# Second batch of a local-attention and token-mixer kernel: half of x, and the first pair, turned by VectorE and DMA; weights of the token map split ahead of x, low halves shared with VectorE

## The chip, the cores and the metric

The kernel runs on one core of a Trainium2 chip. The metric is device time in microseconds: 560.84 us for the kernel before, the median of 3 runs (560.51 to 561.32). The profile is of one execution; its times are counted from the start of its span. Engines: PE is TensorE (PEld its weight loads), DVE VectorE, ACT ScalarE, POOL GpSimd, SP the queue that issues every DMA of this kernel.

## The reference

Windowed attention with summary keys for 4 batches of 8 heads, and behind it a mixer block: one linear map pair across the 768 tokens, one across the 512 channels.

```
scores_l = q @ k.T / 8, masked to |i - j| < 16         # per batch and head, S = 768, D = 64
scores_s = q @ blockmax32(k).T / 8 + log(32)
a = softmax([scores_l, scores_s]);  x = a @ [v, blockmean32(v)]     # heads side by side: 768 x 512
h = relu(x.T @ w_tok1) @ w_tok2                        # 768 -> 256 -> 768 along the tokens
u = x + h.T
out = u + relu(u @ w_ch1) @ w_ch2                      # 512 -> 1536 -> 512 along the channels
```

## The kernel before

**Tiles.** Heads go in pairs: pair p of batch b has number 4 b + p (names such as k_7 or av_16 count pairs or heads over all batches, others count batch, half and pair: up_1_0_2 is batch 1, half 0, pair 2). A batch's tokens fall into two halves, 512 and 256 wide (384 and 384 in the last batch). x lies with tokens on the partitions, x2 holding two pairs of heads; the mixer across channels needs u with channels on the partitions. So x must be turned somewhere between.

**Precision.** Every large product is made of three: an operand is split into a high part (ACT, a copy to a shorter form) and a low part (a subtraction on POOL or DVE), and high x high, high x low and low x high are summed in PSUM.

**Steps of a batch.** `scores` (sc) and `lowest`/`power` give e; `turn` turns e on PE in batches 0 and 1, `turn_blocks` does it in batches 2 and 3 with one 32x32 transpose on DVE, a write to DRAM (away) and four fetches (eT); `weighted` (av) gives x2. The first token map (t1q) runs in `tok1x` for batch 1, two pairs at a time, and in `tok1_all` for batches 2 and 3. `tok2` is the second token map (up): in batches 0 and 1 it first turns x on PE against an identity, into the same PSUM bank, four 128x128 pieces for half 0 and two for half 1; in batches from FAR = 2 on, x comes turned through `turn_x` (DVE transpose xb, write xaway) and `fetch_x` (four fetches xT), and DVE adds the PSUM result to it. `ch1` (hp) and `ch2` (acc) are the channel maps, twelve blocks f of twelve matmuls each for either half, `finish` adds u and writes out.

**Order.** Batch b's channel maps run while batch b+1's attention runs between them. Every piece of work is handed to a `Plan` with an engine, an assumed duration, what it reads and writes, and a rank; the planner plays them through and writes each engine's instructions in the order that comes out. So a change of durations or needs moves instructions on all five engines. Each engine then executes its list strictly in that order, waiting on semaphores. SP issues the DMAs in order too, and a DMA there may also wait until an older DMA has landed.

**Buffers.** A slot has a tag with so many buffers, taken in turn; the first writer of a slot waits until the users of the slot that many places before it are done. Those that matter here: `e` (3), `u0` (4), `ot` (2), and `vb` (1), whose loads in_vb are summed by DVE into vs_2, the block means of batch 2. In PSUM, `att` has two banks; in half 0 the scores, weighted sums and second token map of the next batch share these two, in half 1 they also use acc2 and acc3.

Of the kernel before, what the change touches and what calls it, by code (L numbers as in the profile page):

```python
# [21 lines left out]
DTOK = 256  # L22
# [177 lines left out]
def tile_attention_mixer(  # L200
# [443 lines left out]
    def att_step(b, s, behind=()):  # L644

        kind, hp, g = (LATER if b >= FAR else ORDER)[s]
        p = b * NP + hp
        if kind == "e":
            (turn_blocks if b >= FAR else turn)(p, g)
        elif kind == "a":  # L650
            weighted(p)
            if b >= FAR:
                turn_x(b, hp)
            ahead = 1 if b > 0 else 2
            if b > 0 or hp + ahead < NP:
                load_v(2 * (p + ahead))
                load_v(2 * (p + ahead) + 1)
        else:
            scores(p, g, behind)
            if b == 0 and g == 1:  # L660
                first_means(p)
            if g == 0 and p != NP - 1:
                key_blocks(p + 1)
            if g == 1 and p + 2 < (NP if b == 0 else B * NP):
                load_k(p + 2)
                state["q"] = load_q(p + 2)
# [4 lines left out]
    def turn_x(b, p):  # L671

        x2, a = x_t[b, p]
        e = sbuf([P, S], "e", f"xb_{b}_{p}", 3)
        add(
            "dve", 1.05,
            lambda: nc.vector.transpose(
                e.t.rearrange("p (r t s) -> p t r s", r=P // 32, s=32),
                x2.t[:, :, a, :].rearrange("p t (r s) -> p t r s", s=32),
            ),  # L680
            reads=x_keys(b, p), writes=[(e, 0)], rank=R_ATT,
        )
        away = xa_t[b, p] = plan.slot(dram, [P, S], F32, "xaway", f"xaway_{b}_{p}", 8)
        add(
            "sp", 0.4, lambda: nc.sync.dma_start(out=away.t, in_=e.t),
            reads=[(e, 0)], writes=[(away, 0)], kb=393,
        )

    def fetch_x(b, half, p):
        nt, away = HT[b][half], xa_t[b, p]  # L690
        ts = slice(H0[b][half] // P, (H0[b][half] + nt) // P)
        if b == B - 1:
            slot, behind = sums_at(half, p), state["turned"]
        else:
            tag, bufs = (("e", 3), ("ot", 2))[half]
            slot = xT_t[b, half, p] = sbuf([P, nt], tag, f"xT_{b}_{half}_{p}", bufs)
            behind = ()
        fetch(
            away, slot,
            lambda rows: away.t.rearrange("(q p) (r t s) -> p r q t s", p=32, r=P // 32, s=32)[  # L700
                :, rows.start // 32, :, ts
            ],
            from_sources, nt // 8, behind,
        )
# [114 lines left out]
    def tok1_all(b):  # L819

        pts = [att_bank(f"t1q_{b}_{k}") for k in range(DTOK // P)]
        xk = [key for p in range(NP) for key in x_keys(b, p)]
        for T in range(TT):
            if T % 2 == 0:
                ws = sbuf([P, 2, 2, DTOK], "u0", f"ws_{b}_{T}", 4, F32R)
                split(ws, lambda ws=ws: (ws.t[:, 0], ws.t[:, 1]), [
                    lambda T=T: (slice(None), wt1.t[:, T : T + 2])
                ], [(wt1, T // 2)])
            xs = sbuf([P, 2, NP, P], "u0", f"xs_{b}_{T}", 4, F32R)
            split(xs, lambda xs=xs: (xs.t[:, 0], xs.t[:, 1]), [  # L830
                lambda T=T, g=g: (slice(2 * g, 2 * g + 2), x2_t[b, g].t[:, T]) for g in range(2)
            ], xk)

            def products(T=T, xs=xs, ws=ws):
                for k, pt in enumerate(pts):
                    for i, (wp, xp) in enumerate(((0, 0), (0, 1), (1, 0))):
                        nc.tensor.matmul(  # L837
                            pt.t.rearrange("p (a c) -> p a c", c=P),
                            lhsT=ws.t[:, wp, T % 2, k * P : (k + 1) * P], rhs=xs.t[:, xp],
                            start=(T == 0 and i == 0), stop=(T == TT - 1 and i == 2),  # L840
                        )

            add(
                "pe", 1.37, products, reads=[(s, i) for s in (xs, ws) for i in range(2)],
                writes=[(pt, 0) for pt in pts], rank=R_ATT,
            )
        for p in range(NP):
            t1 = t1_t[b, p] = sbuf([P, 2, DTOK], "t1", f"t1_{b}_{p}", 4, F32R)
            for k, pt in enumerate(pts):
                cs = slice(p * P, (p + 1) * P)  # L850
                to = slice(k * P, (k + 1) * P)
                add(
                    "act", 0.3,
                    lambda t1=t1, pt=pt, cs=cs, to=to: nc.scalar.activation(
                        t1.t[:, 0, to], pt.t[:, cs], AF.Relu
                    ),
                    reads=[(pt, 0)], writes=[(t1, (0, k))], rank=R_EVAC,
                )
                add(
                    "dve", 0.3,  # L860
                    lambda t1=t1, pt=pt, cs=cs, to=to: nc.vector.scalar_tensor_tensor(
                        out=t1.t[:, 1, to], in0=pt.t[:, cs], scalar=0.0,
                        in1=t1.t[:, 0, to].bitcast(F32), op0=ALU.max, op1=ALU.subtract,
                    ),
                    reads=[(pt, 0), (t1, (0, k))], writes=[(t1, (1, k))], rank=R_EVAC,
                )

    def split(slot, parts, sources, keys):

        for source in sources:  # L870
            add(
                "act", 0.62 / len(sources),
                lambda source=source: nc.scalar.activation(
                    parts()[0][:, source()[0]], source()[1], AF.Copy
                ),
                reads=keys, writes=[(slot, 0)], rank=R_EVAC,
            )
        for source in sources:
            add(
                "pool", 1.3 / len(sources),  # L880
                lambda source=source: nc.gpsimd.tensor_tensor(
                    out=parts()[1][:, source()[0]], in0=source()[1],
                    in1=parts()[0][:, source()[0]].bitcast(F32), op=ALU.subtract,
                ),
                reads=keys + [(slot, 0)], writes=[(slot, 1)], rank=R_EVAC,
            )

    def t1_keys(b, p):
# [877 lines left out]
    for b in range(B - 1):  # L1766
# [11 lines left out]
        for slot, (half, f) in enumerate(seq):  # L1778
            state["phase"] = half
            for p in range(NP):  # L1780
                if b >= FAR and u1s[p] == slot + 2:
                    fetch_x(b, 1, p)
                if u1s[p] == slot:
                    tok2(b, 1, p)
# [39 lines left out]
                tok1x(b + 1, t1s.index(slot))  # L1824
            for p in range(NP):
                if slot == t2s[p]:
                    if b + 1 >= FAR:
                        fetch_x(b + 1, 0, p)
                    tok2(b + 1, 0, p)
            if b + 2 == B and slot == 23:  # L1830
# [66 lines left out]
```

## Time and profile before

| | |
|---|---|
| median of 3 runs | 560.84 us |
| the profiled execution | 559.61 us |
| its span, first to last instruction | 557.8 us |
| mean granted TensorE clock | 1.000 |
| POOL busy | 246.8 us (44%) |
| DMA, mean over the span | 181 GB/s, 101.10 MB |
| batch 0's channel maps, from hp_0_0_0 | 64.2 us |
| batch 1's, from hp_1_0_0 | 199.7 us |
| batch 2's, from hp_2_0_0 | 330.7 us |
| last batch's, from z | 466.6 us |

The page gives busy time by engine and the costliest groups of instructions (line, engine, operation, out<-in, count, busy us, mean ns). Rows of a timeline have the start in us, the length in us, engine, line, operation and tiles, a count where neighbours are merged, and in brackets the idle time before it and what ended it. Matmuls overlap in the pipeline, so the length of one is its latency; what it costs is the distance to the next start. Rows of a wait view have engine and line, what was waited for, us in sum, times, and the longest. Rows of the windows view have the stretch, then busy us and instruction count of PE, PEld, DVE, ACT and POOL, the granted clock, the DMA share and GB/s.

### The profile page before, as it was taken

To read this page: it belongs to the slowest core of one execution; us is meant where nothing else is said; L and a number is where in the kernel's file an instruction comes from. 1 tells how busy PE (TensorE), PEld (TensorE's weight loads), DVE (VectorE), ACT (ScalarE), POOL (GpSimd) and SP (SyncE) were. 2 spreads that over 40 slices of the span, in tenths; PEclk is the share of its full clock that TensorE was granted. 3 is DMA by queue.
4 is the path that set the end of the run, shared out by engine and by line. 5 is a ranking of instruction groups with operands and counts; after the bars stand their busy time and mean duration, and the time that the engine had idled before them with its cause. 6 is when DMAs were issued, how large, how long until landed. Compare 5 with 4: busy or idle time off the path is not lost.

```text
span 557.8 us, 12595 instructions
## 1 busy us (share of the span) xinstructions
PE 544.0 (98%) x4557; PEld 479.6 (86%) x4557; DVE 330.3 (59%) x922; ACT 251.9 (45%) x784; POOL 246.8 (44%) x362
## 2 busy tenths in 40 slices
PE   7699999999999999999999999999999999999997
PEld 4588788888999978888799988878889999999997
DVE  4788999979365355454543247454352065669992
ACT  4786666625585344332323325343433453356410
POOL 0326687835574932310067404378769963000000
PEclk9999999999999999999999999999999999999999
DMA  8963668755668138768595316787696543932742
GB/s 277 330 189 108 215 209 249 240 163 190 203 187 251 42 131 226 198 207 226 146 253 137 104 29 196 160 237 198 171 259 168 135 155 116 333 95 81 219 134 85
DMA packets 125743, 101.10 MB, mean 181 GB/s; under 512 B 70000, under 2 KB 105456, under 8 KB 125680
## 3 DMA queue, kind: packets, MB, share of 16 engines
q1 hardware_dynamic: 125680, 100.29, 60.7%
q8 instruction: 36, 0.59, 0.5%
q14 instruction: 27, 0.22, 0.1%
HBM read 70.18 MB, written 28.31 MB: 177 GB/s over the span
## 4 chain that ended last, share of the span: by engine, by line
PE 90%; ACT 4%; DVE 3%; POOL 2%; issue 1%; ACTq 0%
PE acc L1024 27%; PE hp L981 27%; PE sc L467 4%; PE av L599 4%; PE up L920 3%; PE t1q L837 3%; ACT e L491 2%; PE x L1251 2%; PE y L1251 2%; PE z L1251 2%; PE pz L1251 2%; PE t1q L800 2%; PE up L1213 2%; PE warm L1731 1%; PE pw L1251 1%; PE pv L1251 1%
## 5 line engine op out<-in xcount | busy, mean ns | idle before, releaser
L1024 PE MATMUL acc<-h,w2h 128*128 128x256 f32 (+1 forms) x576 | 153.8, 339 | 0.0
L981 PE MATMUL hp<-u,w1h 128*128 128x256 f32 (+1 forms) x576 | 143.8, 339 | 0.0
L1024 PEld LDWEIGHTS acc<-h,w2h 128*128 128x128 f32 x576 | 100.6, 188 | 13.8 <-ACT h L993 1.6
L981 PEld LDWEIGHTS hp<-u,w1h 128*128 128x128 f32 x576 | 98.0, 189 | 12.4 <-issue 1.1
L981 PE MATMUL hp<-u,w1l 128*128 128x256 f32 (+1 forms) x288 | 96.9, 336 | 0.0
L491 ACT ACTIVATE e<-e,den 128x120 f32<-128x120 f32 x192 | 73.3, 384 | 52.0 <-DVE den L481 39.1
L1024 PE MATMUL acc<-h,w2l 128*128 128x256 f32 (+1 forms) x288 | 96.4, 335 | 0.0
L998 DVE SCALAR_TENSOR_TENSOR h<-hp,h 128x512 fp32r<-128x512 f32 (+1 forms) x72 | 39.9, 554 | 90.9 <-ACT h L993 90.7
L993 ACT ACTIVATE h<-hp 128x512 fp32r<-128x512 f32 (+1 forms) x72 | 35.2, 489 | 114.7 <-PE hp L981 114.5
L981 PEld LDWEIGHTS hp<-u,w1l 128*128 128x128 f32 x288 | 54.4, 189 | 5.8
L1024 PEld LDWEIGHTS acc<-h,w2l 128*128 128x128 f32 x288 | 54.2, 188 | 5.2
L481 DVE CUSTOM_DVE_ANT_0 e<-sc,mask_sb 128x120 f32<-128x120 f32 x192 | 41.7, 277 | 16.8 <-PE sc L467 16.2
L605 POOL TENSOR_SCALAR rec<-den 128x6 f32<-128x6 f32 x32 | 8.6, 269 | 66.1 <-ACT e L491 64.0
L491 ACT ACTIVATION_READ_ACCUMULATOR e<-e,den 128x1 f32 x192 | 36.1, 188 | 0.0
L1064 POOL TENSOR_TENSOR ot<-ot,u 128x512 f32<-128x512 f32 (+1 forms) x24 | 24.4, 1042 | 19.7 <-DVE ot L1056 18.2
L467 PE MATMUL sc<-k,q 64*64 64x120 f32 x768 | 28.0, 271 | 3.7 <-DVE den L481 2.2
L467 PEld LDWEIGHTS sc<-k,q 64*64 64x64 f32 x768 | 20.5, 132 | 12.5 <-issue 6.2
L920 PE MATMUL up<-wt2h,t 128*128 128x512 f32 (+1 forms) x96 | 28.4, 354 | 0.6 <-DVE t L739 0.6
L599 PEld LDWEIGHTS av<-v,eT 120*64 120x64 f32 x768 | 24.0, 138 | 4.7 <-issue 2.8
L599 PE MATMUL av<-v,eT 120*64 120x64 f32 x768 | 26.5, 224 | 0.9 <-PE hp L981 0.4
L335 DVE TENSOR_REDUCE ks<-k 128x24 f32<-128x768 f32 x16 | 15.2, 948 | 20.5 <-DMA k<-in_kw 20.5
L423 DVE TENSOR_REDUCE vs<-vb 96x8 f32<-96x256 f32 (+1 forms) x40 | 17.8, 458 | 9.4 <-DMA vb<-in_vb 9.3
(248 smaller groups left out, 1042.7 us busy)
## 6 DMA issues: line engine op xcount, KB each, us to landing
w<-in_w_ch SPq DMA_DIRECT2D x48, 256.0 KB
k<-in_kw SPq DMA_DIRECT2D x16, 720.0 KB
v<-in_vw SPq DMA_DIRECT2D x32, 288.0 KB
q<-in_q SPq DMA_DIRECT2D x16, 384.0 KB
away<-e SPq DMA_DIRECT2D x16, 384.0 KB
eT<-away SPq DMA_DIRECT2D x64, 96.0 KB
w<-in_w_tok SPq DMA_DIRECT2D x12, 256.0 KB
vb<-in_vb SPq DMA_DIRECT2D x32, 96.0 KB
```

The costliest lines, as they stand in the source:

```text
L423: lambda: nc.vector.tensor_reduce(out=s.t[:VB, rows], in_=slot.t[:VB], axis=AX, op=ALU.add),
L467: nc.tensor.matmul(tiles[j].t[c * QT : (c + 1) * QT, i * NC : (i + 1) * NC], lhsT=qt.t[rows, t * QT : (t + 1) * QT], rhs=kt.t[rows, t, :], ...
L481: nc.vector.tensor_tensor_reduce(out=e.t[:, j, i * P : i * P + NC], in0=tiles[j].t[:, i * NC : (i + 1) * NC], in1=mask_sb[:, mv, :], op0=A ...
L491: nc.scalar.activation(ei, ei, AF.Exp, bias=den_t[n].t[:, 1, T : T + 1], scale=-1.0, accum_out=den_t[n].t[:, 0, T : T + 1],)
L599: nc.tensor.matmul(pv[cs, T], lhsT=eT[:NC, T % (TT // 2), cs], rhs=v.t[:NC, 2 * T + c], start=True, stop=True,)
L920: nc.tensor.matmul(pt.t[:, :nt], lhsT=t1.t[:, part, ks], rhs=w.t[:, k, h0 : h0 + nt], start=(far and k == 0 and i == 0), stop=(k == DTOK / ...
L981: nc.tensor.matmul(pt.t[:, :nt], lhsT=block(w, f, c), rhs=us[c].t[:, part], start=(i == 0), stop=(i == len(ops) - 1),)
L993: lambda: nc.scalar.activation(h.t[:, 0], pt.t[:, :nt], AF.Relu),
L998: lambda: nc.vector.scalar_tensor_tensor(out=h.t[:, 1], in0=pt.t[:, :nt], scalar=0.0, in1=h.t[:, 0].bitcast(F32), op0=ALU.max, op1=ALU.sub ...
L1024: nc.tensor.matmul(slot.t[:, c0 : c0 + nt], lhsT=block(w, f, o), rhs=h.t[:, part], start=(f == 0 and w == "w2h" and part == 0 and o % n == 0),
L1064: lambda view=view, u=u: nc.gpsimd.tensor_tensor(out=view(), in0=view(), in1=u.t[:, 1].bitcast(F32), op=ALU.add),
L1251: nc.tensor.matmul(pt.t[:, :cols], lhsT=w[wp][0](), rhs=z.t[:, zp], start=first and seen == 0, stop=final and seen == 3 * len(ops) - 1, sk ...
```

## The change

For batch 1, all four pairs now go through `turn_x`, but pairs 1 to 3 with tokens 512 to 767 alone (two of six 128-token pieces, T0 = 4), pair 0 with all six. `fetch_x` brings half 1 of all four pairs and half 0 of pair 0 back. In `tok2` of batch 1 these five groups lose their turning matmuls on PE and take the branch of the far batches. In `tok1_all` (batches 2 and 3) the weights of the second third are split before x of the first is, the pieces for x carry their own keys for each two pairs, and the low half of pairs 2 and 3 is made by DVE, that of pairs 0 and 1 by POOL as before.

```diff
         elif kind == "a":
             weighted(p)
-            if b >= FAR:
+            if b > 0:
                 turn_x(b, hp)
...
     def turn_x(b, p):
         x2, a = x_t[b, p]
-        e = sbuf([P, S], "e", f"xb_{b}_{p}", 3)
+        T0 = 0 if b >= FAR or (b, p) == (1, 0) else H0[b][1] // P
+        n = (TT - T0) * P
+        tag, bufs = ("vb", 1) if T0 else ("e", 3) if b >= FAR else ("u0", 4)
+        e = sbuf([P, n], tag, f"xb_{b}_{p}", bufs)
         add(
-            "dve", 1.05,
+            "dve", spent(n, 0.4, 0.73),
             lambda: nc.vector.transpose(
                 e.t.rearrange("p (r t s) -> p t r s", r=P // 32, s=32),
-                x2.t[:, :, a, :].rearrange("p t (r s) -> p t r s", s=32),
+                x2.t[:, T0:, a, :].rearrange("p t (r s) -> p t r s", s=32),
             ),
...
-        for T in range(TT):
-            if T % 2 == 0:
-                ws = sbuf([P, 2, 2, DTOK], "u0", f"ws_{b}_{T}", 4, F32R)
...
-            ], xk)
+        def inputs(T):
+            xs = xs_t[T] = sbuf([P, 2, NP, P], "u0", f"xs_{b}_{T}", 4, F32R)
+            split(xs, lambda: (xs.t[:, 0], xs.t[:, 1]), [
+                lambda g=g: (slice(2 * g, 2 * g + 2), x2_t[b, g].t[:, T]) for g in range(2)
+            ], [x_keys(b, 2 * g) + x_keys(b, 2 * g + 1) for g in range(2)], ("pool", "dve"))
+
+        for of, i in (
+            (weights, 0), (inputs, 0), (weights, 1), (inputs, 1), (inputs, 2), (inputs, 3),
+            (weights, 2), (inputs, 4), (inputs, 5),
+        ):
+            of(i)
...
-                if b >= FAR and u1s[p] == slot + 2:
+                if b and u1s[p] == slot + 2:
                     fetch_x(b, 1, p)
...
-                    if b + 1 >= FAR:
+                    if b + 1 >= FAR or (b, p) == (0, 0):
                         fetch_x(b + 1, 0, p)
                     tok2(b + 1, 0, p)
```

What the planner makes of it is shown at three places. On PE, the first group of the second token map of batch 1, up_1_0_0 (t1_1_0 is its input from the first map, wt2h and wt2l the weights' parts, identf the identity), in the program before:

```order
L912 MATMUL up_1_0_0_2724<-identf_66,x_1_0_2007 128x128 x4
L920 MATMUL up_1_0_0_2724<-wt2h_687,t1_1_0_2693 128x512
L920 MATMUL up_1_0_0_2724<-wt2l_705,t1_1_0_2693 128x512
L920 MATMUL up_1_0_0_2724<-wt2h_687,t1_1_0_2693 128x512 x2
L920 MATMUL up_1_0_0_2724<-wt2l_705,t1_1_0_2693 128x512
L920 MATMUL up_1_0_0_2724<-wt2h_687,t1_1_0_2693 128x512
L912 MATMUL up_1_0_1_2741<-identf_66,x_1_0_2007 128x128 x4
```

and in the changed one:

```order
L940 MATMUL up_1_0_0_2731<-wt2h_687,t1_1_0_2701 128x512
L940 MATMUL up_1_0_0_2731<-wt2l_705,t1_1_0_2701 128x512
L940 MATMUL up_1_0_0_2731<-wt2h_687,t1_1_0_2701 128x512 x2
L940 MATMUL up_1_0_0_2731<-wt2l_705,t1_1_0_2701 128x512
L940 MATMUL up_1_0_0_2731<-wt2h_687,t1_1_0_2701 128x512
L932 MATMUL up_1_0_1_2743<-identf_66,x_1_0_2007 128x128 x4
```

The four turning matmuls of up_1_0_0 are gone, those of up_1_0_1 to up_1_0_3 stay; each up_1_1 group loses its two in the same way.

On DVE, in the second half of batch 0, between the reduction of block 4 of the channel map (h_0_1_4) and that of block 5: ks_7 is the block maximum of the keys k_7, whose load is under way, and e_6_0 the first reduction of the scores of pair 6 (sc_12, sc_13). Before:

```order
L998 SCALAR_TENSOR_TENSOR h_0_1_4_2085<-hp_0_1_4_2045,h_0_1_4_2085 128x256
L423 TENSOR_REDUCE vs_2_1649<-vb_2_7_2043 96x8
L625 RECIPROCAL rec_10_2096<-rec_10_2096 128x6
L625 RECIPROCAL rec_11_2106<-rec_11_2106 128x6
L335 TENSOR_REDUCE ks_7_2138<-k_7_2061 128x24
L344 COPY k_7_2061<-ks_7_2138 128x12x24
L998 SCALAR_TENSOR_TENSOR h_0_1_5_2154<-hp_0_1_5_2123,h_0_1_5_2154 128x256
L481 ISA e_6_0_2170,den_12_2171<-sc_12_0_2140,mask_sb_71 128x120
```

In the changed program, from the last of the e_6_0 reductions on:

```order
L481 ISA e_6_0_2171,den_13_2176<-sc_13_0_2143,mask_sb_71 128x120
L481 ISA den_13_2176 128x1
L335 TENSOR_REDUCE ks_7_2197<-k_7_2065 128x24
L344 COPY k_7_2065<-ks_7_2197 128x12x24
L1018 SCALAR_TENSOR_TENSOR h_0_1_6_2217<-hp_0_1_6_2184,h_0_1_6_2217 128x256
L610 TENSOR_TENSOR x_1_0_2007<-av_10_2203,rec_10_2099 128x6x64
L610 TENSOR_TENSOR x_1_0_2007<-av_11_2219,rec_11_2107 128x6x64
```

ks_7 and its copy have moved behind the e_6_0 reductions and stand ahead of the scalings of av_10 and av_11. The transpose xb_1_0 stands some 25 rows ahead of this place, and on SP its write xaway_1_0 stands ahead of the load of k_7.

On SP, in the first half of batch 1's channel maps, where the turned e of pair 8 (first pair of batch 2) is written and fetched. Before:

```order
L556 DMA away_8_0_2969<-e_8_0_2557 128x768
L292 DMA vb_3_0_3007<-in_vb 96x256
L556 DMA away_8_1_3019<-e_8_1_2605 128x768
L574 DMA eT_8_0_3054<-away_8_0_2969 32x24x32 x4
L292 DMA vb_3_1_3061<-in_vb 96x256
L574 DMA eT_8_1_3076<-away_8_1_3019 32x24x32 x4
```

and now:

```order
L556 DMA away_8_0_2997<-e_8_0_2608 128x768
L292 DMA vb_3_0_3020<-in_vb 96x256
L556 DMA away_8_1_3043<-e_8_1_2613 128x768
L574 DMA eT_8_0_3067<-away_8_0_2997 32x24x32 x4
L574 DMA xT_1_1_2_3101<-xaway_1_2_2875 32x4x64 x4
L292 DMA vb_3_1_3106<-in_vb 96x256
L574 DMA eT_8_1_3108<-away_8_1_3043 32x24x32 x4
```

The fetch of turned x (xT_1_1_2) has come between the two fetches of pair 8. On PE the weighted sums of pair 8 (av_16, av_17), which read these, stand now behind block 4 of the first channel map (hp_1_0_4), before ahead of it. The two other fetches of half 1 stand earlier and later on SP, and the buffer vb, single, is used on DVE in the order: sum of vb_2_11, transpose xb_1_1, sums of vb_2_12 to vb_2_15, transpose xb_1_2, and, behind the four ot_0_1 additions, transpose xb_1_3.

More of the change, by code (lines that the diff above doesn't have):

```diff
@@ L682, in turn_x @@
         )
-        away = xa_t[b, p] = plan.slot(dram, [P, S], F32, "xaway", f"xaway_{b}_{p}", 8)
+        away = plan.slot(dram, [P, n], F32, f"xaway{n}", f"xaway_{b}_{p}", 8)
+        xa_t[b, p] = away, T0
         add(
             "sp", 0.4, lambda: nc.sync.dma_start(out=away.t, in_=e.t),
-            reads=[(e, 0)], writes=[(away, 0)], kb=393,
+            reads=[(e, 0)], writes=[(away, 0)], kb=n * 512 / 1000,
         )
     def fetch_x(b, half, p):
-        nt, away = HT[b][half], xa_t[b, p]
-        ts = slice(H0[b][half] // P, (H0[b][half] + nt) // P)
+        nt, (away, T0) = HT[b][half], xa_t[b, p]
+        ts = slice(H0[b][half] // P - T0, (H0[b][half] + nt) // P - T0)
         if b == B - 1:
@@ L822, in tok1_all, with weights @@
         xk = [key for p in range(NP) for key in x_keys(b, p)]
-        for T in range(TT):
-            if T % 2 == 0:
-                ws = sbuf([P, 2, 2, DTOK], "u0", f"ws_{b}_{T}", 4, F32R)
[L826 to L831, printed above, removed]
-            ], xk)
+        ws_t, xs_t = {}, {}
+        def weights(c):
+            ws = ws_t[c] = sbuf([P, 2, 2, DTOK], "u0", f"ws_{b}_{c}", 4, F32R)
+            split(ws, lambda: (ws.t[:, 0], ws.t[:, 1]), [
+                lambda: (slice(None), wt1.t[:, 2 * c : 2 * c + 2])
+            ], [[(wt1, c)]])
+        def inputs(T):
[8 more added lines that the diff above has]
+            of(i)
+            if of is weights:
+                continue
+            T, xs, ws = i, xs_t[i], ws_t[i // 2]
             def products(T=T, xs=xs, ws=ws):
@@ L843, in tok1_all @@
             add(
-                "pe", 1.37, products, reads=[(s, i) for s in (xs, ws) for i in range(2)],
+                "pe", 1.37, products,
+                reads=[(xs, (i, g)) for i in range(2) for g in range(2)] + [(ws, (i, 0)) for i in range(2)],
                 writes=[(pt, 0) for pt in pts], rank=R_ATT,
@@ L866, in tok1_all, with split @@
                 )
-    def split(slot, parts, sources, keys):
-        for source in sources:
+    def split(slot, parts, sources, keys, engs=("pool",)):
+        n = len(sources)
+        for g, source in enumerate(sources):
             add(
-                "act", 0.62 / len(sources),
+                "act", 0.62 / n,
                 lambda source=source: nc.scalar.activation(
@@ L875, in split @@
                 ),
-                reads=keys, writes=[(slot, 0)], rank=R_EVAC,
+                reads=keys[g], writes=[(slot, (0, g))], rank=R_EVAC,
             )
-        for source in sources:
+            eng = engs[g]
             add(
-                "pool", 1.3 / len(sources),
-                lambda source=source: nc.gpsimd.tensor_tensor(
+                eng, (1.3 if eng == "pool" else 0.8) / n,
+                lambda source=source, eng=eng: (
+                    nc.gpsimd if eng == "pool" else nc.vector
+                ).tensor_tensor(
                     out=parts()[1][:, source()[0]], in0=source()[1],
@@ L884, in split @@
                 ),
-                reads=keys + [(slot, 0)], writes=[(slot, 1)], rank=R_EVAC,
+                reads=keys[g] + [(slot, (0, g))], writes=[(slot, (1, g))], rank=R_EVAC,
             )
```

## The prediction

> **What bounds the kernel now.** I read the first two parts of the page, then the waits of PE, then PE's timeline at the places that the change touches.
>
> ```profile
> span 557.8 us, 12595 instructions
> ...
> PE 544.0 (98%) x4557; PEld 479.6 (86%) x4557; DVE 330.3 (59%) x922; ACT 251.9 (45%) x784; POOL 246.8 (44%) x362
> ```
>
> PE is busy for 98% of the span. A busy share proves little by itself, so the next view asks what PE waits for between 66 us, where the first mixer block runs, and the end.
>
> ```profile
> engine line waited for: us in total, times, longest us
> PE av L599 <- PE hp L981: 0.4, 1, 0.4
> ```
>
> One wait of 0.4 us in 492 us. So from 66 us on, the time is the sum of PE's own matmuls plus a tail behind the last one that no edit touches. Two things follow. An edit saves what it takes out of PE's stream plus at most that one wait, and nothing else. And an edit costs something only where it makes PE wait for what it did not wait for before. What happens on DVE, ACT, POOL and SP counts only through such waits.
>
> **What leaves PE.** The change takes 12 turning matmuls (L912) out of batch 1: four in up_1_0_0 and two in each up_1_1 group. Their mean of 274 ns is a latency in a pipeline, not a cost; the cost is read from the distance between starts.
>
> ```profile
> 186.65 0.60 PE L912 MATMUL up<-identf,x 128*128 128x128 f32 x4
> 187.01 0.51 PE L920 MATMUL up<-wt2h,t 128*128 128x512 f32 x1
> ...
> 188.53 0.60 PE L912 MATMUL up<-identf,x 128*128 128x128 f32 x4
> ...
> 320.86 0.40 PE L920 MATMUL up<-wt2h,t 128*128 128x512 f32 x1
> ...
> 326.46 0.28 PE L1024 MATMUL acc<-h,w2h 128*128 128x256 f32 x1
> ```
>
> Group up_1_0_0 with its turning runs from 186.65 to 188.53: 1.88 us. Batch 2 runs the same group without turning already: four of them from 320.86 to 326.46, 1.40 us each. Saved: **0.48 us**. Of this the four turnings are 0.36, and the rest is the first product behind them, 0.34 to the next start where 0.23 is usual.
>
> ```profile
> 209.94 0.38 PE L912 MATMUL up<-identf,x 128*128 128x128 f32 x2
> 210.08 0.37 PE L920 MATMUL up<-wt2h,t 128*128 128x256 f32 x1
> ...
> 210.88 0.63 PE L981 MATMUL hp<-u,w1h 128*128 128x512 f32 x2
> ...
> 342.33 0.28 PE L920 MATMUL up<-wt2h,t 128*128 128x256 f32 x1
> ...
> 343.04 0.63 PE L981 MATMUL hp<-u,w1h 128*128 128x512 f32 x2
> ```
>
> A half-1 group takes 0.94 with two turnings and 0.71 without: 0.23 less, four times, **0.92 us**. Together 1.40. The groups of scores and weighted sums change places with whole blocks, but each still has one block ahead and one behind; I count 0 for that, and 0.1 either way in the range.
>
> **How much PE can use of it.** POOL makes the low halves of the inputs for t1q_1_1, the first linear map of pairs 2 and 3, in a row without gaps; its last piece is read by the second dozen of the products at 190.36.
>
> ```profile
> 190.33 1.30 POOL L786 TENSOR_TENSOR ws<-wt,ws 128x512 fp32r<-128x512 f32 x1
> 190.36 1.83 PE L800 MATMUL t1q<-xs,ws 128*128 128x256 f32 x14
> ```
>
> POOL ends at 191.63. Twelve products of 256 columns take 1.43 (0.12 each, as in the half-1 group above), and the third of the second dozen is the first to read that piece: 190.36 + 1.43 + 0.24 = 192.03. PE comes 0.48 earlier now, at 191.55, while POOL's row began before the saving. So PE waits for about **0.1 us** here.
>
> **The wait that there is.** It stands in the first pair's region.
>
> ```profile
> 156.25 1.62 PE L599 MATMUL av<-v,eT 120*64 120x64 f32 x48 [0.39 <-PE hp L981]
> ...
> 158.57 0.87 PE L529 MATMUL et<-identf,e 128*120 128x128 f32 x6
> ...
> 153.51 0.95 DVE L335 TENSOR_REDUCE ks<-k 128x24 f32<-128x768 f32 x1 [2.87 <-DMA k<-in_kw]
> ...
> 155.06 0.27 DVE L481 CUSTOM_DVE_ANT_0 e<-sc,mask_sb 128x120 f32<-128x120 f32 x1
> ...
> 146.52 0.37 SPq L292 DMA_DIRECT2D k<-in_kw  x1
> ```
>
> The page names hp, which had long ended. DVE stood 2.87 us for the keys k_7, issued at 146.52, with the six reductions of e_6_0 behind it; only these free the bank that av_10 writes. In the changed order the reductions stand ahead of ks_7, so this wait goes. What is late next: av_10 and av_11 are now scaled behind ks_7, and et_12_0 needs their bank, at 158.57 in this trace, 158.2 without the wait. ks_7, its copy and the h behind it took 153.51 to 155.06, 1.55. The keys are later, since xaway_1_0 (393 KB) is issued ahead: some 0.4 us of issue, as the load itself took, and 1.5 us of transfer at the 254 GB/s that the next row has for these 5 us.
>
> ```profile
> 145.00:150.00 5.00, 5.00 (x61) 4.71 (x60) 1.73 (x13) 3.26 (x15) 1.11 (x3) 1.00 0.85 254
> ```
>
> 153.5 + 1.9 + 1.55 gives 157.0. A scaling that frees a bank is worth some 0.5 (two thirds of the 0.69 that a 512-column add takes below), so the banks are free at 157.5 and 158.0, and et_12_0 at 158.2 does not wait. The margin is 0.2 to 0.7, so I take **-0.3 us**; the bounds are -0.4 (no wait) and +0.6 (keys 1.3 us later still).
>
> **What is added, and its cover.** In batch 2 the same steps stand already: the transpose, the add out of PSUM, and the low half, which goes to POOL in half 1.
>
> ```profile
> L677 DVE STREAM_TRANSPOSE xb<-x x8: 978/978/980, 226.2 to 430.4; 128x768 f32<-128x768 f32 x8
> ...
> L936 DVE TENSOR_TENSOR xT<-up,xT x8: 414/554/691, 322.5 to 368.9; 128x512 f32<-128x512 f32 x4, 128x256 f32<-128x256 f32 x4
> ...
> L950 POOL TENSOR_TENSOR u<-xT,u x4: 734/738/746, 344.7 to 370.2; 128x256 fp32r<-128x256 f32 x4
> ...
> 211.82 0.39 DVE L964 TENSOR_TENSOR u<-up,u 128x256 fp32r<-128x256 f32 x1
> ```
>
> DVE gets one transpose of 0.98 and three of 128x256, which no row has: between a third of 0.98 and all of it, I take 0.35, nearest to a cost that goes by size. It gets adds of 0.69 and four times 0.41, and gives four subtractions of 0.39 to POOL, where they take 0.74: in sum 2.0 + 2.3 - 1.6 = 2.7 us more. The first row below has 9.2 us of DVE in the 22 us that matter; its load fits, the risk is its order.
>
> ```profile
> 186.00:208.00 22.00, 22.00 (x171) 18.80 (x171) 9.19 (x28) 8.71 (x24) 14.15 (x16) 1.00 0.26 89
> ...
> 188.98 0.42 DVE L423 TENSOR_REDUCE vs<-vb 96x8 f32<-96x256 f32 x1 [2.58 <-DMA vb<-in_vb]
> 191.44 0.42 DVE L423 TENSOR_REDUCE vs<-vb 96x8 f32<-96x256 f32 x1 [2.04 <-DMA vb<-in_vb]
> ...
> 199.99 0.69 DVE L964 TENSOR_TENSOR u<-up,u 128x512 fp32r<-128x512 f32 x1 [1.14 <-ACT u L959]
> ...
> 205.19 0.09 DVE L481 DVE_READ_ACCUMULATOR2_ANT den<- 128x1 f32 x1
> ...
> 199.73 0.63 PE L981 MATMUL hp<-u,w1h 128*128 128x512 f32 x2
> ...
> 206.31 0.84 PE L467 MATMUL sc<-k,q 64*64 64x120 f32 x24
> ```
>
> xb_1_1 to xb_1_3 share one buffer (vb, one slot) with the loads that vs_2 sums. A round of that buffer is 2.46 us (188.98 to 191.44) and DVE waits through it. xb_1_1 puts the last four sums one round later, so DVE now waits with u_1_0_0, t1_1_2 and u_1_0_3 behind it. In this trace u_1_0_3 ends at 200.68 and the product that reads it starts at 202.0, ten steps of 0.23 into hp_1_0_0 (199.73): 1.3 us ahead. PE comes 0.7 earlier (0.38 and 0.3), but so does up_1_0_3. The four sums follow from about 189, behind the add of xT_1_0_0, at 2.46 a round: the fourth near 197 to 199, with SP's three fetches of xT_1_1_0 (0.46 each, 1.85 for four below) ahead of its load; so u_1_0_3 ends at 200 to 201, against 201.3. I take 0, and +1 as the other bound. xb_1_3 must moreover wait until xaway_1_2 has landed, with h_1_0_0 and the e_8_0 reductions behind it. These end at 205.28 here, 1.0 ahead of the second scores of pair 8; xb_1_3 takes 0.35 of that. 0 again, same bounds.
>
> On SP, xT_1_1_2 now stands between eT_8_0 and eT_8_1.
>
> ```profile
> 217.91 2.66 SPq L574 DMA_DIRECT2D eT<-away  x4
> ...
> 223.84 1.62 PE L599 MATMUL av<-v,eT 120*64 120x64 f32 x48
> ...
> 345.46 1.85 SPq L574 DMA_DIRECT2D xT<-xaway  x4
> ...
> 347.41 6.34 SPq L574 DMA_DIRECT2D eT<-away  x8
> ...
> 355.78 1.62 PE L599 MATMUL av<-v,eT 120*64 120x64 f32 x48
> ```
>
> Four fetches issue in 1.85 us, so the last of eT_8_1 moves from 220.57 to 222.4. av_16 moves too, behind hp_1_0_4: a block of twelve products of 0.23 later, 2.8, less 0.46 of turning ahead of it: 226.2. That leaves 3.8 us; batch 2 had 2.0 (353.75 to 355.78) and PE did not wait. Cost 0.
>
> [...]
>
> For batches 2 and 3 the weights of tok1_all are split earlier and six low halves each go from POOL (0.75 each) to DVE. PE had no wait there, so nothing can be gained: 0. Cost: the first low half now stands behind x of pair 3 and its transpose on DVE.
>
> ```profile
> 298.10 1.62 PE L599 MATMUL av<-v,eT 120*64 120x64 f32 x48
> ...
> 300.36 0.98 DVE L677 STREAM_TRANSPOSE xb<-x 128x768 f32<-128x768 f32 x1
> ```
>
> The transpose starts 0.64 behind av_23 (299.72); with 0.98 and 0.39 the low half is there 2.0 behind it, and the products start two blocks of twelve at 0.12 behind it, 2.9. Cost 0, and +0.5 as the far bound.
>
> **The sum.** -1.40 + 0.1 - 0.3 = -1.6 us. The profiled execution took 559.61 (span 557.8), so 558.0 by it. The median of the runs is 560.84, 1.23 above the profiled one; I carry the difference over: **559.2 us**, 0.29% less. About 0.2%, 1.1 us, is what a measurement of this kernel can tell from no change.
>
> **The rivals.**
> - *DVE in order (within 0.2%).* A sum that waits for its load, or xb_1_3 for its own transfer, stands ahead of u_1_0_3, h_1_0_0 or the reductions, and PE waits at hp_1_0_0 or at the second scores of pair 8, or the keys k_7 hold et_12_0. For: margins of 0.3 to 1 us against a round of 2.46. Against: DVE is idle more than half of the stage. Price 0.5 to 1.5: 559.7 to 560.7.
> - *Late fetches (slower).* If 20 fetches and 4 writes more delay eT, av_16 and then av_18 wait. It decides once the last eT_8_1 issues 1.8 us later than worked out (3.8 less the 2.0 of batch 2); to be slower by more than 0.2% it needs 2.7 us of waiting over the four weighted sums of the stage: 562 to 564. For: SP issues in order and each fetch waits for an older one. Against: batch 2 carries the same load. [...]
> - *PE gains nothing (within 0.2%).* The turnings filled time in which weights were loaded anyway. For: PEld is busy for 86% of the span. Against: the groups without turning are shorter in the rows above. 560.8.
>
> **How the numbers follow.** Forecast (558.7 to 559.7) 0.56; DVE in order 0.28; nothing gained 0.06; late fetches 0.10. All of the first lies beyond 0.2%; the second and third within, except that its lower edge touches the bound. So faster 0.56, within 0.34, slower 0.10. Range: from 558.6 (no wait anywhere, -0.4 and nothing lost at POOL, with 0.3 for the turnings' spread and the runs) to 561.3, which takes in the second and third rivals and leaves out the slower one.
>
> **What would show it.** In the profile after: up_1_0_0 in 1.40 and each up_1_1 group in 0.71; no L599 wait near 155 and none at et_12_0; a wait of about 0.1 at t1q_1_1; no PE wait at hp_1_0_0, at the scores of pair 8 or at av_16. PE's busy time falls by some 1.4. A PE wait on DVE between 190 and 206 speaks for the first rival; one on DMA eT at L599 for the second. The prediction is wrong if PE waits in sum over 0.5 us from 66 us on, or if the groups without turning do not reach batch 2's lengths.

## The result, and the profile after

The changed kernel takes **567.94 us**, the median of 6 runs (564.98 to 568.97); the kernel before took 560.67 beside it (6 runs, 559.22 to 561.32). The ratio is 1.0124, 95% interval 1.0097 to 1.0151: the change costs about 7 us, where 1.6 us less than before were forecast. The profiled execution took 566.36 us against 559.61, so it holds 6.75 of this difference. Its page, span and busy time by engine:

```profile
span 564.6 us, 12660 instructions
...
PE 547.6 (97%) x4545; PEld 482.7 (85%) x4545; DVE 344.3 (61%) x939; ACT 253.0 (45%) x784; POOL 242.5 (43%) x354
```

PE has its 12 matmuls less (4545 against 4557), yet is busy for 3.6 us more. So part of the loss lies inside matmuls, and the busy row can't tell where. The waits of PE between 66 us and the end (waited for; us in sum, times, longest) tell the other part:

```profile
PE t1q L853 <- POOL xs L901: 3.3, 1, 3.3
PE av L599 <- DMA eT<-away: 0.3, 1, 0.3
```

Before, there was one wait of 0.4. The new one of 3.3 us is not in batch 1, on which the prediction spent its care, but in the first token map of batch 3, at the third of its three dozens of products, the one for the last third of the tokens (T = 4 and 5). PE's timeline there, after:

```profile
449.79 0.39 PE L853 MATMUL t1q<-xs,ws 128*128 128x512 f32 x1
453.45 4.23 PE L853 MATMUL t1q<-xs,ws 128*128 128x512 f32 x11 [3.27 <-POOL xs L901]
457.48 0.58 PE L1001 MATMUL hp<-u,w1h 128*128 128x256 f32 x2
```

and before:

```profile
446.75 2.91 PE L837 MATMUL t1q<-xs,ws 128*128 128x512 f32 x12
449.50 0.28 PE L1024 MATMUL acc<-h,w2h 128*128 128x256 f32 x1
```

Twelve products took 2.75 us from start to next start; now they take 7.69. Of the 4.94 more, 3.27 are the wait. The rest is in the rows themselves: eleven products need 4.03 us to the next start, 0.37 each, where twelve needed 0.23 each. The windows of the changed kernel (busy us and count of PE, PEld, DVE, ACT, POOL, then granted clock, DMA share, GB/s) say why:

```profile
446.00:450.00 4.00, 4.00 (x35) 3.86 (x33) 1.18 (x3) 0.79 (x3) 0.00 (x0) 1.00 0.72 207
450.00:454.00 4.00, 0.73 (x3) 0.48 (x3) 0.00 (x0) 0.00 (x0) 3.77 (x4) 1.00 0.43 155
454.00:458.00 4.00, 4.00 (x13) 3.21 (x12) 0.29 (x1) 0.57 (x3) 3.84 (x6) 0.57 0.00 0
458.00:462.00 4.00, 4.00 (x32) 4.00 (x31) 2.34 (x9) 2.16 (x8) 1.04 (x2) 1.00 0.00 0
```

Behind the wait the granted clock is 0.57 for a window, and then 1.00 again. And through the whole window ahead of it POOL does nothing at all, though PE is about to wait for POOL. POOL's timeline, after:

```profile
439.89 1.29 POOL L1156 TENSOR_TENSOR wc_w_None<-wc_w_None,wa_w_None 128x512 fp32r<-128x512 f32 x1
450.23 1.26 POOL L1115 TENSOR_TENSOR wa_w_None<-w2h,w2l 128x512 f32<-128x512 f32 x1 [9.05 <-DMA mix_w2h<-wa_w_None]
451.45 1.26 POOL L901 TENSOR_TENSOR ws<-wt,ws 128x512 fp32r<-128x512 f32 x1
452.67 1.43 POOL L901 TENSOR_TENSOR xs<-x,xs 128x256 fp32r<-128x256 f32 x2
```

POOL stands for 9.05 us until a DMA lands, for a piece of the last batch's mixer weights (w2_4, the sum of w2h and w2l into the buffer wa_w) that nobody needs soon; behind it stand the low halves ws and xs that PE waits for. They could have run: ACT had the high half of ws long done.

```profile
440.38 0.63 ACT L891 ACTIVATE ws<-wt 128x512 fp32r<-128x512 f32 x1
```

The DMA for which POOL stands sits on SP's queue behind a row of fetches (its row is the second; it issues at 447.25):

```profile
443.17 4.04 SPq L574 DMA_DIRECT2D uf<-xaway  x6
447.25 0.43 SPq L1172 DMA_DIRECT2D mix_w2h<-wa_w_None  x1
```

Before, POOL waited for this DMA too, but behind its last low halves:

```profile
443.29 2.85 POOL L881 TENSOR_TENSOR xs<-x,xs 128x256 fp32r<-128x256 f32 x4 [1.24 <-ACT xs L873]
448.49 2.54 POOL L1095 TENSOR_TENSOR wa_w_None<-w2h,w2l 128x512 f32<-128x512 f32 x2 [2.35 <-DMA mix_w2h<-wa_w_None]
```

There 2.35 us of waiting cost nothing, for nothing of PE's stood behind it. The order of POOL's instructions shows the exchange. Before:

```
L881 TENSOR_TENSOR ws_3_4_5722<-wt1_392,ws_3_4_5722 128x512
...
L881 TENSOR_TENSOR xs_3_5_5783<-x_3_1_5263,xs_3_5_5783 128x256
L1095 TENSOR_TENSOR wa_w2_4_None_5812<-w2h_1_1202,w2l_1_1208 128x512
L1095 TENSOR_TENSOR wa_w2_4_None_5812<-w2h_3_1537,w2l_3_1557 128x512
```

After:

```
L1115 TENSOR_TENSOR wa_w2_4_None_5798<-w2h_1_1202,w2l_1_1208 128x512
L901 TENSOR_TENSOR ws_3_2_5796<-wt1_392,ws_3_2_5796 128x512
L901 TENSOR_TENSOR xs_3_4_5800<-x_3_0_4716,xs_3_4_5800 128x256
L901 TENSOR_TENSOR xs_3_5_5815<-x_3_0_4716,xs_3_5_5815 128x256
L1115 TENSOR_TENSOR wa_w2_4_None_5798<-w2h_3_1537,w2l_3_1557 128x512
```

(ws_3_4 before and ws_3_2 after are the same weights, those of the last third; the name counts tokens before and thirds after.) In the program text these weights stand where they stood, between the inputs of T = 3 and of T = 4; what the diff moved is the weights ahead of them and the low halves' engine, and with that the planner's times. In these the mixer piece and the low half of the last weights became ready within about 0.2 us of each other, and the piece went first, though its rank is the last of all: a rank decides only between works that are ready at the same moment. Which of the two, the weights' new place or the low halves' engine, moves these times was not separated.

### The profile page after: what moved, and what is told of

Same layout as the page of the kernel before. It is cut to its first block, busy times and chain, and to the rows that moved or that the text cites. A ratio compares the mean times of both kernels' runs of the same rounds, so it can differ in the third digit from the quotient of the medians.

```text
span 564.6 us, 12660 instructions
## 1 busy us (share of the span) xinstructions
PE 547.6 (97%) x4545; PEld 482.7 (85%) x4545; DVE 344.3 (61%) x939; ACT 253.0 (45%) x784; POOL 242.5 (43%) x354
## 4 chain that ended last, share of the span: by engine, by line
PE 82%; POOL 4%; SPq 4%; DMA 3%; DVE 3%; ACT 3%; issue 1%; POOLq 0%
PE hp L1001 24%; PE acc L1044 23%; PE av L599 4%; PE sc L467 4%; PE up L940 3%; SPq L574 3%; PE x L1271 2%; PE y L1271 2%; PE z L1271 2%; PE pz L1271 2%; PE t1q L853 2%; PE t1q L804 2%; ACT e L491 2%; PE up L1233 1%; PE et L529 1%; PE pw L1271 1%
## 5 line engine op out<-in xcount | busy, mean ns | idle before, releaser
L599 PEld LDWEIGHTS av<-v,eT 120*64 120x64 f32 x768 | 25.6, 144 | 4.8 <-issue 3.6
L599 PE MATMUL av<-v,eT 120*64 120x64 f32 x768 | 28.4, 231 | 0.7 <-DMA eT<-away 0.3
```

The source lines that it names most:

```text
L599: nc.tensor.matmul(pv[cs, T], lhsT=eT[:NC, T % (TT // 2), cs], rhs=v.t[:NC, 2 * T + c], start=True, stop=True,)
```

## The experiments

The expectations name the theories by letters and give what each expects. Theory A is the reading above: the order of POOL's instructions at the third dozen of batch 3's token map, with the half clock behind it, makes nearly all of the loss, and the rest of the change is worth next to nothing. All ratios are to the kernel before, run beside each group of experiments on the same chip.

**The two parts apart.** The change has a part that turns x of batch 1 and a part in `tok1_all`. The first kernel has only the turning; `tok1_all` and `split` are those of before.

```diff
-        for of, i in (
-            (weights, 0), (inputs, 0), (weights, 1), (inputs, 1), (inputs, 2), (inputs, 3),
-            (weights, 2), (inputs, 4), (inputs, 5),
-        ):
...
+        for T in range(TT):
+            if T % 2 == 0:
+                ws = sbuf([P, 2, 2, DTOK], "u0", f"ws_{b}_{T}", 4, F32R)
```

> Only the turning of batch 1 (x of tokens 512 to 767 and pair 0 through VectorE and DMA); the token map of batches 2 and 3 as before. Theory A (the loss is GpSimd's row at the third token map: a mixer piece that waits for a DMA stands ahead of the last low halves, PE waits 3.4 us and then runs 3.8 us at half clock): no PE wait on POOL near 450, time 560 to 561.5, within 0.2% of before. Theory B (the turning loads SP and the DMA queues, and so makes the DMA late that GpSimd waits for): 565 us or more, with a wait of about 3 us near 450.

Measured: 560.51 us, ratio 1.0006 (0.9985 to 1.0027). There is no wait on POOL, so the turning isn't what makes POOL's DMA late (theory B); PE waits for the turned e instead, its one row from 66 us on:

```profile
PE av L599 <- DMA eT<-away: 2.5, 3, 1.2
```

So the turning alone neither gains nor costs what can be measured: in its profile, what PE saves it waits for later. The second kernel has only the other part.

```diff
-            if b > 0:
+            if b >= FAR:
                 turn_x(b, hp)
...
-                if b and u1s[p] == slot + 2:
+                if b >= FAR and u1s[p] == slot + 2:
                     fetch_x(b, 1, p)
...
-                    if b + 1 >= FAR or (b, p) == (0, 0):
+                    if b + 1 >= FAR:
                         fetch_x(b + 1, 0, p)
```

> Only the token map of batches 2 and 3 changed (weights split ahead, low halves of pairs 2 and 3 on VectorE); batch 1 turned on PE as before. Theory A: the PE wait on POOL of some 3.4 us near 449 is there and the clock falls to 0.5 behind it; time 560.7 + 5.3 = 566, at least 564.5. Theory B: no such wait, 560 to 561.5.

Measured: 565.4 us, ratio 1.0096 (1.006 to 1.0131). The loss is here, with no x of batch 1 turned at all. Its waits on POOL, and the window behind the wait:

```profile
PE t1q L849 <- POOL xs L897: 2.5, 1, 2.5
```

```profile
450.00:454.00 4.00, 2.77 (x13) 2.31 (x14) 0.29 (x1) 0.28 (x1) 3.92 (x6) 1.00 0.00 0
```

In the profiled execution the wait was 2.5 us and the clock stayed at 1.00 behind it; that execution was also the fastest of six (562.55 at a mean clock of 0.994, the others 565 to 569 at 0.987 to 0.991). So this wait of 2.5 us was followed by no half clock, where that of 3.3 us in the changed kernel was (0.57); which of the other five runs had the half clock here is not shown, since one execution is profiled.

**The order alone.** The change as it is, with one edge more in the planner: the mixer piece must come behind the last low half that POOL makes for batch 3.

```diff
+        if b == B - 1:
+            state["mix", "w2", 4, 0].behind.update(state["low"])
...
-            add(
+            low = add(
...
+            if eng == "pool":
+                state["low"] = [low]
```

> The whole change, with one order edit: the first GpSimd piece of the mixer weights w2_4 (wa_w2_4, which waits for a DMA) is planned behind the last low half of the third token map. Theory A: PE's wait near 450 and the half clock behind it are gone, 5.3 us less than the changed kernel: 561 to 563. Rival C (the low halves are late in any case, since their weights are split late, or the delayed mixer pieces hold the last batch instead): the time stays at 565 or more and PE waits near 450 on ACT, or behind 466 on a DMA or POOL.

Measured: 560.89 us, ratio 1.0005 (0.9981 to 1.0028). One edge takes back the whole loss. POOL's timeline, and PE's row of the third dozen:

```profile
442.21 1.29 POOL L903 TENSOR_TENSOR ws<-wt,ws 128x512 fp32r<-128x512 f32 x1 [0.48 <-ACT ws L893]
...
445.90 0.74 POOL L903 TENSOR_TENSOR xs<-x,xs 128x256 fp32r<-128x256 f32 x1 [0.57 <-ACT xs L893]
451.16 2.55 POOL L1119 TENSOR_TENSOR wa_w_None<-w2h,w2l 128x512 f32<-128x512 f32 x2 [4.51 <-DMA mix_w2h<-wa_w_None]
```

```profile
449.50 2.91 PE L853 MATMUL t1q<-xs,ws 128*128 128x512 f32 x12
```

The low halves end at 446.6, three us ahead of PE. POOL still waits for the DMA, 4.51 us and until 451.16, later than in the changed kernel; it costs nothing. What costs is what stands behind a wait, not its length.

**Wait and clock apart.** The change as it is, with 15 products of a zero tile added on PE within the wait (they add nothing to the sums).

```diff
+                for _ in range(15 if (b, T) == (B - 1, 4) else 0):
+                    nc.tensor.matmul(
+                        pts[0].t, lhsT=zero, rhs=wt2h.t[:, 0, :512], start=False, stop=False
+                    )
```

> The whole change, and 15 more products with a zero matrix (512 columns, 0.23 us each, 3.45 in all) on PE just ahead of the products that wait for POOL near 450; they add zeros. Theory A's second half (PE standing still is what drops the clock): the clock stays at 1.0 there, and the time is 1.9 us less than that of the changed kernel, 565.5 to 566.5. Rival D (the clock falls for another reason, or the wait is costlier than it looks): no change, 567 to 569, with the clock at 0.5 behind 450 as before.

Measured: 564.72 us, ratio 1.0067 (1.0048 to 1.0086). Its windows over the same stretches:

```profile
450.00:454.00 4.00, 4.00 (x20) 3.20 (x19) 0.00 (x0) 0.00 (x0) 3.75 (x4) 1.00 0.40 148
454.00:458.00 4.00, 4.00 (x26) 3.58 (x25) 1.27 (x5) 1.26 (x6) 3.84 (x6) 1.00 0.00 0
```

The clock stays at 1.00 and some 2 to 3 us come back (1.0124 for the change, 1.0104 in its repeat below, less 1.0067 is 0.4 to 0.6%), a little more than the 1.9 expected; the interval overlaps that of the repeat, so the clock's share rests on the windows more than on these ratios. What stays, 3.7 us by the ratio, is about the wait itself: the 15 zero products, which now fill it, take 3.5 us at the 0.23 us that a 512-column product took before.

**The change once more,** unedited, to see whether its wait belongs to every group of runs.

> The changed kernel once more, beside the others on one chip, so that its wait and its clock are known from a second profile. If the wait near 450 belongs to the order of GpSimd's row, it is there again, 2.5 to 4.5 us, with or without a half clock behind it; time 1.0% to 1.5% above before. If it was chance, it is gone and the time is that of e3, 560 to 561.

Measured: 567.15 us, ratio 1.0104 (1.0072 to 1.0135); the same wait, and the half clock behind it:

```profile
PE t1q L853 <- POOL xs L901: 3.3, 1, 3.3
```

```profile
454.00:458.00 4.00, 4.00 (x10) 3.13 (x11) 0.04 (x1) 0.28 (x1) 3.84 (x6) 0.50 0.00 0
```

**Why nothing is gained even with the order mended.** The kernel with the edge should be 1 to 1.5 us faster than before by the forecast. In its profile 1.1 us of waits on the turned e are back (two, the longest 0.9). The next two kernels start from it and try to take these away, first by moving the weighted sums of the first heads of batches 2 and 3, av_16 and av_24, behind block 3 of ch2:

```diff
+    for b in (1, 2):
+        state["av", (b + 1) * H].behind.add(state["acc", b, 0, 3])
```

> e3 (mixer piece behind the last low half), and the weighted sums av_16 and av_24 one block of PE later (behind the second channel map of block 3). Theory E (the 1.8 us that turning and the k_7 wait give back are eaten by PE waiting for fetched eT at av_16 and av_24, 0.4 and 1.2 us in e3): no wait on DMA eT there, 1 to 1.6 us less than e3, that is 0.1% to 0.3% below before. Rival F (the fetches are later still, or the delay passes on to the scaling, the transposes and up_2_0): waits at av_18, av_20, t1q_2 or up_2_0 instead, time as e3, 0.0% to 0.1% above before.

Measured: 560.86 us, ratio 1.0004 (0.9988 to 1.002). The waits at av_16 and av_24 are gone, but not the time, of which 1 to 1.6 us less than with the edge alone was expected; other waits stand in their place:

```profile
PE av L599 <- DMA eT<-away: 0.7, 2, 0.5
PE hp L1005 <- DVE u L974: 0.7, 1, 0.7
PE sc L467 <- DVE xT L960: 0.6, 1, 0.6
PE t1q L853 <- POOL xs L903: 0.4, 1, 0.4
```

Then by the queue: the fetch of turned x that had come between the two fetches of pair 8 goes behind both, and av_16 behind block 4 of ch1.

```diff
+    for w in state["xT", 1, 1, 2]:
+        w.behind.update(state["eT", 8, 1])
+    state["av", 16].behind.add(state["hp", 1, 0, 4])
```

> e3, with the fetch xT_1_1_2 behind the fetch eT_8_1 on SP, and av_16 kept behind hp_1_0_4 on PE. If SP's order makes eT_8_1 late (four fetches, 2.0 us ahead of it), av_16 does not wait (e3: 0.3 us of 0.38) and up_1_1_2 may; the wait at av_24 stays at 0.5 to 1.2. If the transfer itself is late (the DMA engines are busy, whoever is issued first), av_16 waits as before. Time within 0.1% of e3 in either case; the answer is in the profile.

Measured: 562.21 us, ratio 1.0035 (1.0014 to 1.0056): slower than without the edit, a miss.

```profile
PE av L599 <- DMA eT<-away: 2.1, 2, 1.5
```

av_16 waits no longer, so it was SP's order that made it wait; but the heads behind it now wait longer, av_20 by 1.65 us. The last added fetch has been issued at 227.9 here, 46 us ahead of av_20 (274.25), so the added DMAs don't stand in front of that head in the queue; by what way the turning makes it late is not shown.

**The start.** The changed kernel's profile shows a half clock at 18 to 21 and 31 to 35 us (0.51 and 0.57), where its instructions are those of before. 14 products of zeros near 28 and 30 us were added to the kernel with the later weighted sums, to fill PE's gaps there.

```diff
+                    for _ in range({2: 6, 4: 8}.get(T, 0) if (b, p, k) == (0, 0, 0) else 0):
+                        nc.tensor.matmul(
+                            pt.t[:, :P], lhsT=fz, rhs=x2.t[:, 0, a, :], start=False, stop=False
+                        )
```

> e5, and 14 products that add zeros in the first map of pair 0 (six ahead of the third, eight ahead of the fifth product, 0.11 us each), where PE waits 1.0 and 1.3 us for the weights near 28 and 30 us. If PE standing still is what drops the clock in the first 40 us, there is no half clock from 31 to 35 us any more and the time is 0.3 to 1 us less than e5 in the median, less scattered. If the clock falls for another reason, the half clock near 31 us comes as often as in e5 (in three of the five profiles so far) and the time is that of e5.

Measured: 563.72 us, ratio 1.0067 (1.0041 to 1.0093): slower than without the products, and inconclusive on the clock. (The half clock near 31 us stood in two of the five profiles meant, the changed kernel's and that with the edge.) Its profile has no half clock between 30 and 40 us (1.00), but neither has that of the kernel without the products (1.00); and PE got waits on DVE that this one lacked:

```profile
PE acc L1054 <- DVE h L1028: 1.2, 1, 1.2
PE et L531 <- DVE x L612: 0.7, 1, 0.7
```

The order of the rest is unchanged. One constant tile more also moves the buffers behind it; whether that is the cause was not tried.

**How much turning pays.** Three kernels with `tok1_all` as before. One turns pair 0 of batch 1 alone:

```diff
-            if b > 0:
+            if b >= FAR or (b, hp) == (1, 0):
                 turn_x(b, hp)
```

> Of the change only pair 0 of batch 1 (both halves) is turned by VectorE and DMA: 8 fetches and one write more than before instead of 20 and 4, the token map as before, PE's order that of before without six turning matmuls. Theory E (what the turning gives back is eaten by late fetches of eT, and these come from 20 fetches on SP and from weighted sums that moved): the waits at av_16 to av_24 stay under 0.2 us each, and PE gains 0.47 + 0.23 + 0.45 (wait at av_10) = 1.1 us: 0.2% below before. Rival G (any fetch more costs as much): as before or slower.

Measured: 560.11 us, ratio 0.9993 (0.9978 to 1.0009). up_1_0_0 is 0.46 us shorter, and 0.2 of it is waited for again at t1q_1_1; a quarter-microsecond each is lost at av_20 and at up_1_1_0. Less than the 1.1 us expected, and by the time as rival G had it: the 1.1 held 0.45 for the wait of before at av_10, and this is no gain of an edit (below). The next turns the second half of all four pairs, and no first half:

```diff
-        T0 = 0 if b >= FAR or (b, p) == (1, 0) else H0[b][1] // P
+        T0 = 0 if b >= FAR else H0[b][1] // P
```

> The four pairs of batch 1 for tokens 512 to 767 alone (16 fetches, 4 small writes), pair 0 of tokens 0 to 511 turned by PE as before, token map as before. Theory E: PE saves 4 x 0.22 = 0.9 us, and av_16, av_20 or av_24 wait 0.5 to 2 us together for fetched eT: 0.1% below to 0.2% above before. Rival G: above before by 0.2% or more.

Measured: 564.14 us, ratio 1.0061 (1.0041 to 1.0081).

```profile
PE av L599 <- DMA eT<-away: 2.8, 3, 1.6
PE acc L1028 <- DVE h L1002: 0.6, 1, 0.6
```

These groups save 0.92 us of PE at most, and PE waits 2.8 us for turned e: slower by more than 0.2%, again as rival G had it. But this kernel differs from the one before it in two things, 16 fetches in place of 8 and the buffer of the transposes (`vb`, shared with the loads for vs_2, in place of `u0`), so the fetches themselves and the shared buffer are not told apart. The last is the kernel before with the 12 turning matmuls left out and nothing put in their place (so x is missing from those five groups, and the output lacks it there): what the turning costs in all.

```diff
-            for i in range(0 if far else nt // P):
+            left_out = b == 1 and (half == 1 or p == 0)
+            for i in range(0 if far or left_out else nt // P):
```

> The kernel before with the 12 turning matmuls of batch 1 left out and nothing in their place: x is then missing in u of batch 1, tokens 512 to 767, and of pair 0, tokens 0 to 511. It measures what the turning costs on PE at most. By the distance between starts it is 0.47 + 4 x 0.22 = 1.35 us: 0.24% below before. If the turnings fill time in which weights are loaded anyway, nothing.

Measured: 559.79 us, ratio 0.9982 (0.9964 to 1.0000). In its profile the groups lose 0.47 and four times 0.22, and 0.2 come back as a wait at t1q_1_1. And its one row from 66 us on is a wait for turned e, at av_24, though this kernel adds no DMA and keeps the order of before:

```profile
PE av L599 <- DMA eT<-away: 0.2, 1, 0.2
```

The row of av_24 and av_25 takes 1.92 us to the next start, where before it took 1.55: 0.4 more. SP had issued the last fetch for it 1.7 us ahead (before: 2.0), having taken 6.59 us for the eight of them in place of 6.34. So this wait can come without the added DMAs, and 0.8 to 1.2 us, 0.2%, bound what turning these five groups elsewhere could have won, with the rest of the kernel as it is.

## Why the prediction was wrong, by its steps

The two profiled executions, compared by the starts of the same matmuls:

| step | forecast | measured |
|---|---|---|
| turning leaves PE | -1.40 | -1.35 |
| wait on POOL at t1q_1_1 | +0.1 | +0.2 |
| wait at av_10, and small ones near 168 us | -0.3 | -0.7, not by the change |
| late eT at av_16, 18, 20, 24 | 0 | +1.4 |
| scores sc_18 | 0 | +0.4 |
| `tok1_all`: wait in batch 3 | 0 (far bound +0.5) | +3.4 |
| half clock behind it | none | +1.8 |
| half clock at the start | none | +1.6, by chance |
| sum | -1.6 | +6.75 |

**The step that failed** is the one on the token weights: "For batches 2 and 3 the weights of tok1_all are split earlier and six low halves each go from POOL (0.75 each) to DVE. PE had no wait there, so nothing can be gained: 0", with "Cost 0, and +0.5 as the far bound". It looked at the engine that got more work, DVE, in batch 2, and at its first low half alone. The cost arose on the engine that lost work, in the other batch, at the last low halves. The words "PE had no wait there" were true, but a cover has to be named for both engines: in the trace of before, POOL's last xs ended at 446.1, 0.6 us ahead of the third dozen at 446.75, and the next instruction stood 2.35 us for a DMA. Set beside each other, these two rows give the price of an exchange: the piece could not start before 448.49, takes 1.27 (two take 2.54), and a low half of weights behind it some 1.3, so PE, there at 446.75, would have waited until 451.1: over 4 us, by rows of before alone. The order edge (ratio 1.0005 in place of 1.0124) and the part alone (1.0096) show that this is the cause.

**The clock** adds 1.8 us to the 3.4 of the wait, and no step had it: the prediction let the other engines count only through PE's waits, but behind a wait the same matmuls took longer (0.37 us from start to start in place of 0.23). Waits of 3.3 us were followed by windows at 0.57 and then 1.00 in one profile of the change, at 0.50 and then 0.82 in the other; the wait of 2.5 us in the kernel with `tok1_all` alone by 1.00; and the 15 zero products within the wait kept it at 1.00. So here the clock fell where PE stood still for 3.3 us, and held where it stood for 2.5 or was kept busy. At what length of wait it falls is not shown, and a wait of this length is not needed for it: the half clock in the first 40 us of the changed kernel (below) came with no PE wait over 1.6 us.

**Turning** was right in size: PE's timeline after has up_1_0_0 from 187.56 to 188.96, 1.40 us, and an up_1_1 group from 213.31 to 214.02, 0.71, as batch 2 had them. So the third rival, that PE gains nothing, did not come.

```profile
187.56 0.40 PE L940 MATMUL up<-wt2h,t 128*128 128x512 f32 x1
...
188.96 0.60 PE L932 MATMUL up<-identf,x 128*128 128x128 f32 x4
...
213.31 0.28 PE L940 MATMUL up<-wt2h,t 128*128 128x256 f32 x1
...
214.02 0.40 PE L1044 MATMUL acc<-h,w2h 128*128 128x512 f32 x1
```

**Late fetches** were the second rival, and the term that stood at 0 measured 1.4 us. SP's queue and PE's row of av_16 and the next, after:

```profile
218.79 2.02 SPq L574 DMA_DIRECT2D xT<-xaway  x4
220.90 0.38 SPq L292 DMA_DIRECT2D vb<-in_vb  x1
221.32 2.69 SPq L574 DMA_DIRECT2D eT<-away  x4
```

```profile
227.13 1.97 PE L599 MATMUL av<-v,eT 120*64 120x64 f32 x48
229.03 0.50 PE L1044 MATMUL acc<-h,w2h 128*128 128x512 f32 x1
```

The last fetch of eT_8_1 ends its issue at 224.0, not 222.4, and av_16 comes 3.1 us behind it. The step took the 2.0 us of batch 2 as enough; here 3.1 were not. (The rival's own bound, an issue 1.8 us later than worked out, was not reached: it was 1.6.) The wait hides inside the row: 48 small matmuls take 1.90 us to the next start, where before they took 1.55 (223.84 to 225.39); the thirteenth, the first to read the second part of eT, starts late. The wait view lists one of the four such waits (0.3). The other kernels that turn all of it agree: 2.5 us of such waits with the turning alone, 1.1 with the order edge, against 1.35 of matmuls. What makes sc_18 start 0.4 later was not followed. Nor is it shown by what way the turning makes the later heads late. SP has issued the last added fetch at 230.6, but av_18 starts at 251.8, av_20 at 274.9 and av_24 at 356.9; and av_24 waits with the turning merely left out, too. Only for av_16 do the runs show the way: the fetch ahead of eT_8_1 in SP's order.

**The wait at av_10** went, but not for the reason given. It is also absent from the kernels that turn one pair, or second halves alone, or leave the turning out, and the last has the order of before throughout. So the -0.3 was no effect of ks_7's new place; most likely it differs between executions, but the kernel before was profiled once. **DVE in order**, the first rival, did not come: no PE wait on DVE stands between 190 and 206 us. (The transposes of 128x256 took 0.445 us, not 0.35; no wait of PE is listed on them.)

**From the profile to the median.** The forecast carried 1.23 us over from the profiled execution of before. That execution had the clock at 1.00 from the start; the one after did not. Windows of the changed kernel, then of before:

```profile
18.00:21.00 3.00, 3.00 (x79) 2.70 (x76) 1.97 (x5) 1.20 (x7) 0.00 (x0) 0.51 1.07 401
31.00:35.00 4.00, 4.00 (x51) 3.78 (x51) 3.19 (x20) 3.26 (x16) 0.00 (x0) 0.57 0.13 46
```

```profile
18.00:21.00 3.00, 2.65 (x86) 2.25 (x82) 2.28 (x8) 1.99 (x11) 0.00 (x0) 1.00 1.06 397
31.00:35.00 4.00, 4.00 (x114) 3.54 (x117) 3.44 (x20) 3.42 (x18) 0.41 (x2) 1.00 0.53 161
```

The instructions of the first 145 us are the same in both, so 1.6 of the 6.75 us is no work of the change, and neither are the 0.7 of av_10 and behind: 6.75 - 1.6 + 0.7 = 5.85 us, a ratio of 1.0104, which lies within the intervals of both measurements of the change. Carrying the 1.23 over is no part of the error.

No version tried is measurably faster than before. The nearest are the one with a single pair turned (0.9993) and the change with the order edge, with the later weighted sums (1.0004) and without (1.0005); all three intervals include 1.

## What to carry to other kernels

Where a scheduler sets the order, a change that moves work off an engine has to be checked on the engine that lost it as well: look for instructions that wait for a DMA and ask what has come to stand behind them. A wait of an in-order engine is priced by what is queued behind it, not by its length: 4.5 us cost nothing in one order, 9 us cost 5 in the other. With PE as the bound, the wait of 3.4 us in the changed kernel cost half as much again (1.8 us more), since the clock fell to 0.57 behind it; so the clock behind a wait is to be read as well as its length.

## What the runs showed of the hardware

- The half clock also came in the first 40 us of the changed kernel (0.51 and 0.57 in the windows above), and not in the profiled execution of before (1.00 in the same windows). Where it came can be seen in profiled executions alone, but the mean clock of a run tells that it varies: over the three groups of experiments, 81 runs of the unchanged kernel before had a mean granted clock of 0.998 and more in 23 runs (median 559.17 us), 0.993 to 0.997 in 49 (560.45) and 0.991 or less in 9 (562.04). So a profiled execution can stand 1.3 to 2.9 us apart from another of the same kernel; two profiles are compared stretch by stretch, not by their spans.
- Products with a tile of zeros as one operand kept the clock up (1.00 through 450 to 458 us with the 15 of them in the wait; 0.57 from 454 to 458 without).
- Turning a 128x128 block on PE cost 0.09 us by the distance between starts (0.36 for four), a third of the 274 ns that its row gives as the mean of one.
